# One of two inverse matmuls per class replaced by DMA swaps and an addition from batch 2 on, and new steps for the spectral stages

## The chip, the core and the metric

The kernel runs on one core of one Trainium2 chip. The metric is the device time in microseconds (us). The kernel before took 840.69 us (median of 3 runs, 840.57 to 841.27).

## The reference, cut to what matters

```python
# x: (8, 3008, 256) float32; filt_r, filt_i: (1505, 256)
X = np.fft.rfft(x, axis=1)
Y = X * (filt_r + 1j * filt_i)[None]
y = np.fft.irfft(Y, n=3008, axis=1)            # the spectral part, per batch
h = y.reshape(24064, 256) @ w_in               # 256 -> 2048
g = h + np.sin(alpha * h) ** 2 / (alpha + 1e-9)
out = g @ w_out                                # 2048 -> 256: the MLP part
```

## The kernel before: the parts that the change touches

A transform of 3008 = 47 x 64 points is done as matmuls in three stages per batch: stage 1 (`pa`), a DFT over the 47; a trip through DRAM that turns the data round (store `d1` from `t1`, load `t2`); stage 2, for each of 24 classes a forward matmul (`pb`), the filter, an inverse matmul (`pc`); again a trip through DRAM (`d2` from `g`, load `t4`); stage 3 (`pd`), which gives `y`. The MLP runs in 47 chunks of at most 512 columns, 8 steps a chunk. A step is two hidden tiles (`ph`, two 512-column matmuls each), cosine on ScalarE (`cos`), the activation on VectorE (`v`), and eight output matmuls (`po`) of the chunk before. The spectral pieces of batches 1 to 7 are laid between these steps, so that they hide under the MLP. What is written at one step is called a piece. A matmul's result stands in PSUM, TensorE's output memory, until ScalarE or VectorE copies it out; that copy is called an evacuation.

```python
def stage2(u):                       # 13 pieces; two classes in each
    if u < 12:
        ps = ...                     # PSUM
        for i in range(2):
            s = 2 * u + i
            nc.tensor.matmul(out=ps[:, i, :], lhsT=d_t[:, s, :], rhs=st["t2"][s // 6][:, s % 6, :], ...)
        xf = xfpool.tile([128, 2, C], FP16, ...)
        nc.scalar.copy(out=xf, in_=ps)
        for k in range(2):           # real and imaginary filter
            pt = ppool.tile(...)
            nc.vector.tensor_tensor(out=pt, in0=xf, in1=f_t[k][:, 2 * u:2 * u + 2, :], op=ALU.mult)
            pr.append(pt)
        st["p", u] = pr
    if u > 0:
        w = u - 1
        for i in range(2):
            for k in range(2):       # two inverse matmuls per class
                nc.tensor.matmul(out=ps[:, i, :], lhsT=e_t[:, k, 2 * w + i, :], rhs=pr[k][:, i, :],
                                 start=(k == 0), stop=(k == 1))
        evac(...)                    # 1 in 3 on VectorE, else ScalarE
        # ... every third piece: store g to d2

# the step at which each piece is written; pending pieces are sorted by it
plan = {1: [-45 + i for i in range(8)],
        2: [-29 + 14 * i / 13 for i in range(13)],
        3: [-10, -9] + [-7 + 2 * i for i in range(14)]}      # plus 48 * b
```

The lines on an engine do not stand in program order: a scheduler orders them at build time by its own estimate of when each is ready. Each engine then works through its list in that order.

## Time and profile before

| | before |
|---|---|
| time, median | 840.69 us |
| TensorE (PE) busy | 799.8 us, 96% |
| VectorE (DVE) busy | 628.1 us, 75% |
| ScalarE (ACT) busy | 613.0 us, 73% |

The table of 20 us windows has for each engine the busy us in the window with the number of instructions, then the granted TensorE clock, the DMA engines' busy share and GB/s. These windows hold stages 1 and 2 of one batch:

```profile
core 0: us, PE busy (x) PEld busy (x) DVE busy (x) ACT busy (x) POOL busy (x), PEclk, DMA share, GB/s
160.00:180.00 20.00, 19.79 (x137) 12.58 (x135) 14.74 (x24) 16.17 (x34) 1.55 (x3) 1.00 0.60 120
180.00:200.00 20.00, 20.00 (x155) 13.84 (x154) 15.51 (x26) 15.18 (x31) 0.52 (x1) 1.00 0.78 179
200.00:220.00 20.00, 19.89 (x147) 14.17 (x145) 17.62 (x36) 16.15 (x32) 0.00 (x0) 1.00 0.33 76
```

TensorE has no room there; VectorE in stage 2 (200 to 220) is at 88%.

The chain that ended last, as shares of the span by engine and then by line, from the page of the kernel before:

```profile
PE 83%; DMA 7%; ACT 4%; issue 3%; DVE 2%; POOL 0%; SPq 0%; ACTq 0%; DVEq 0%; POOLq 0%
PE po L369 36%; PE ph L354 35%; PE pc L199 4%; PE pa L157 3%; ACT cos L357 2%; PE pd L219 2%; PE pb L180 2%; DMA t<-d 1%; DMA w_out<-in_moe_w_out_dram 1%; DMA d<-g 1%; DMA d_t<-d_tbl 1%; DVE p L187 1%; DMA x<-in_x_dram 1%; DMA filt<-in_filt_i_dram 1%; ACT t L135 1%
```

Most of it, 83%, is TensorE, the two MLP products (`po`, `ph`) alone 71%. The groups of instructions (busy us, mean ns, then the idle time before them and what ended most of it) show what the change goes after:

```profile
L199 PE MATMUL pc<-p,e_t 128*128 128x256 f16 x384 | 59.7, 275 | 2.6 <-DVE p L187 1.5
```

A matmul's listed 275 ns is not its cost, because matmuls overlap. The cost in a busy stream is the distance from one matmul's start to the next: median 109 ns for 128x256 and 216 ns for 128x512, worked out from the start times in the trace. The Trainium skill, "TensorE: Matmul & The Clock Gate", section "Wait — 56ns, not 53.3ns?", gives N / 2.4 GHz plus about 2.5 ns for such a distance. Worked out from that formula, an estimate for N = 256 and 512 is 109.2 and 215.8 ns; the trace agrees. From these distances I made a tally: each distance less the median of its shape is lost time, put down to whatever ended TensorE's idle time before the later matmul.

### The profile page before, as it was taken

Reading aid. Unit: us, or ns where it says so; the run is one execution under the profiler, and the core shown is the slowest. Engines: PE = TensorE matmul, PEld = TensorE weight load, DVE = VectorE, ACT = ScalarE, POOL = GpSimd, SP = SyncE. Lnnn points to the kernel's source line nnn. Section 1 sums busy time; section 2 is a strip of 40 time slices with the busy share of each in tenths; the row PEclk is TensorE's granted clock in tenths of the full one; section 3 lists DMA queues with packets and bytes.
Section 4 is the critical chain, followed back from the end, with each engine's and each line's share of the span. In section 5 each row is a group of like instructions: output and inputs, shape, how many; then the busy total and the mean of one; then the engine's idle time right before and its main releaser. Section 6 shows DMA issues by size and latency. Waiting matters only on the chain.

```text
span 837.2 us, 16122 instructions
## 1 busy us (share of the span) xinstructions
PE 799.8 (96%) x5793; PEld 544.2 (65%) x5793; DVE 628.1 (75%) x1119; ACT 613.0 (73%) x1200; POOL 28.3 (3%) x55
## 2 busy tenths in 40 slices
PE   5758999999999999999999999999999999999996
PEld 2425676667776677666776677666777677666674
DVE  3658886778877788777877788777877778777772
ACT  4536886787868787787877777777877878677763
POOL 3210000000000000000000000000000000000000
PEclk9969999999999999999999999999999999999999
DMA  9985835185344744266242763447443353421111
GB/s 220 218 255 117 200 89 130 51 174 116 82 135 81 171 99 109 75 141 153 65 130 60 165 137 82 115 91 171 92 96 94 97 113 83 115 58 38 38 40 45
DMA packets 93495, 94.98 MB, mean 113 GB/s; under 512 B 8084, under 2 KB 82852, under 8 KB 93416
## 3 DMA queue, kind: packets, MB, share of 16 engines
q1 hardware_dynamic: 84784, 75.02, 34.5%
q0 software_dynamic: 6704, 18.09, 12.5%
q10 hardware_dynamic: 1928, 0.86, 0.5%
q8 instruction: 45, 0.74, 0.3%
q14 instruction: 34, 0.28, 0.1%
HBM read 58.02 MB, written 49.81 MB: 129 GB/s over the span
## 4 chain that ended last, share of the span: by engine, by line
PE 83%; DMA 7%; ACT 4%; issue 3%; DVE 2%; POOL 0%; SPq 0%; ACTq 0%; DVEq 0%; POOLq 0%
PE po L369 36%; PE ph L354 35%; PE pc L199 4%; PE pa L157 3%; ACT cos L357 2%; PE pd L219 2%; PE pb L180 2%; DMA t<-d 1%; DMA w_out<-in_moe_w_out_dram 1%; DMA d<-g 1%; DMA d_t<-d_tbl 1%; DVE p L187 1%; DMA x<-in_x_dram 1%; DMA filt<-in_filt_i_dram 1%; ACT t L135 1%
## 5 line engine op out<-in xcount | busy, mean ns | idle before, releaser
L358 DVE SCALAR_TENSOR_TENSOR v<-cos,ph 128x512 f16<-128x512 f32 (+1 forms) x768 | 484.0, 672 | 164.0 <-ACT cos L357 163.5
L357 ACT ACTIVATE cos<-ph 128x512 f32<-128x512 f32 (+1 forms) x768 | 411.6, 589 | 153.9 <-PE ph L354 152.5
L369 PE MATMUL po<-w,v 128*128 128x256 f16 x3008 | 400.9, 273 | 2.6 <-DVE w L337 2.6
L354 PE MATMUL ph<-y,w 128*128 128x512 f16 (+1 forms) x1536 | 391.5, 377 | 0.2 <-ACT y L135 0.2
L369 PEld LDWEIGHTS <-v 128*128 128x128 f16 x3008 | 289.0, 98 | 80.9 <-issue 8.7
L354 PEld LDWEIGHTS <-w 128*128 128x128 f16 x1536 | 150.4, 98 | 101.0 <-issue 4.6
L187 DVE TENSOR_TENSOR p<-xf,filt 128x512 f16<-128x512 f16 x192 | 72.1, 419 | 4.9 <-ACT xf L183 4.5
L375 ACT COPY o<-po 128x512 f32<-128x512 f32 x96 | 55.6, 579 | 17.7 <-PE po L369 15.5
L135 ACT CAST t<-pa 96x512 f16<-96x512 f32 x89 | 51.0, 589 | 19.0 <-PE pa L157 18.9
L183 ACT CAST xf<-pb 128x512 f16<-128x512 f32 x96 | 57.0, 595 | 8.1 <-PE pb L180 5.5
L219 PEld LDWEIGHTS <-t 96*128 96x128 f16 x512 | 36.3, 100 | 39.8 <-DMA t<-d 11.8
L199 PE MATMUL pc<-p,e_t 128*128 128x256 f16 x384 | 59.7, 275 | 2.6 <-DVE p L187 1.5
L157 PE MATMUL pa<-x,wf_t 94*96 94x512 f16 x128 | 47.2, 408 | 10.1 <-DMA x<-in_x_dram 6.3
L219 PE MATMUL pd<-wi_t,t 96*128 96x94 f16 x512 | 43.4, 208 | 11.1 <-DMA t<-d 10.9
L135 ACT CAST y<-pd 128x376 f16<-128x376 f32 x82 | 39.1, 479 | 12.5 <-PE pd L219 12.5
L199 PEld LDWEIGHTS <-e_t 128*128 128x128 f16 x384 | 37.6, 99 | 15.6 <-issue 7.1
L180 PE MATMUL pb<-t,d_t 128*128 128x256 f16 x192 | 38.2, 283 | 2.5 <-DMA t<-d 1.5
L135 ACT CAST g<-pc 128x512 f16<-128x512 f32 x64 | 38.7, 605 | 1.6 <-PE pc L199 1.6
L137 DVE CAST t<-pa 96x512 f16<-96x512 f32 x39 | 26.6, 683 | 15.8 <-PE pa L157 15.8
L180 PEld LDWEIGHTS <-d_t 128*128 128x128 f16 x192 | 18.9, 101 | 23.8 <-issue 4.6
L118 POOL DMA_DIRECT2D x<-in_x_dram x32 | 16.7, 524 | 502.8 <-PE pa L157 490.5
L157 PEld LDWEIGHTS <-wf_t 94*96 94x96 f16 x128 | 16.6, 129 | 19.6 <-issue 9.9
(28 smaller groups left out, 94.3 us busy)
## 6 DMA issues: line engine op xcount, KB each, us to landing
d<-t SPq DMA_DIRECT2D x32, 384.0 KB
d<-g SPq DMA_DIRECT2D x64, 192.0 KB
t<-d SPq DMA_DIRECT2D x32, 384.0 KB
x<-in_x_dram POOLq DMA_DIRECT2D x32, 376.0 KB, 6.9
t<-d SPq DMA_DIRECT2D x60, 192.0 KB
out_dram<-o SPq DMA_DIRECT2D x72, 94.0 KB
w_in<-in_moe_w_in_dram POOLq DMA_DIRECT2D x2, 1024.0 KB, 9.2
w_out<-in_moe_w_out_dram POOLq DMA_DIRECT2D x1, 2048.0 KB, 11.6
```

Source lines behind the costliest of these rows:

```text
L135: marks["act"] = nc.scalar.copy(out=dst, in_=src)
L157: marks["pe"] = nc.tensor.matmul(out=ps[0:NK, :], lhsT=wf_t, rhs=st["x"][ch][:, n0:n0 + 2, :], start=True, stop=True)
L180: nc.tensor.matmul(out=ps[:, i, :], lhsT=d_t[:, s, :], rhs=st["t2"][s // 6][:, s % 6, :], start=True, stop=True)
L183: nc.scalar.copy(out=xf, in_=ps)
L187: marks["prod", u] = nc.vector.tensor_tensor(out=pt, in0=xf, in1=f_t[k][:, 2 * u:2 * u + 2, :], op=ALU.mult)
L199: nc.tensor.matmul(out=ps[:, i, :], lhsT=e_t[:, k, 2 * w + i, :], rhs=pr[k][:, i, :], start=(k == 0), stop=(k == 1))
L219: nc.tensor.matmul(out=psv[:, i, :], lhsT=st["t4"][:, 4 * half + i, cb * 128:cb * 128 + 128], rhs=wi_t, start=True, stop=True)
L354: nc.tensor.matmul(out=ps[:, 0:n], lhsT=w1[:, cb, jb * 128:jb * 128 + 128], rhs=y_cols[:, cb, c0:c0 + n], start=(cb == 0), stop=(cb == 1))
L357: nc.scalar.activation(out=cs[:, 0:n], in_=ps[:, 0:n], func=AFT.Sin, bias=float(np.pi / 2))
L358: marks["snake"] = nc.vector.scalar_tensor_tensor(out=v[k][:, jb, 0:n], in0=cs[:, 0:n], scalar=-1.0, in1=ps[:, 0:n], op0=ALU.add, op1=ALU. ...
L369: nc.tensor.matmul(out=pso[k][:, t % 2, :], lhsT=v[k][:, jb, 128 * t:128 * t + 128], rhs=w2[:, jb, :], start=(jb == 0), stop=(jb == 15))
L375: nc.scalar.copy(out=o[:, 0:nb, :], in_=pso[k][:, 0:nb, :])
```

## The change

The second inverse matmul of a class has the same weights as the first, with their halves swapped and one half negated. So the two matmuls on `xf * f0` and `xf * f1` can be one on `xf * f0 + swap(xf) * f1'`, where `f1'` holds the swapped, signed filter. The change does that from batch 2 on. The halves of `xf` (real and imaginary, partitions 0 to 63 and 64 to 127) are swapped by two DMAs from GpSimd's queue, in the program's order two pieces ahead of VectorE's use. Stage 2 is spread over 24 steps instead of 14, one evacuation in five instead of one in three goes to VectorE, which has the additions to do, and the load of the next batch's x is written behind the t2 load.

```diff
 def stage2(u):                                  # batches 2 to 7; 15 pieces
+    if u < 12:
+        forward(u)
+        xs = xspool.tile([128, 2, C], FP16, ...)
+        for p in range(2):
+            nc.gpsimd.dma_start(out=xs[64 * p:64 * p + 64, :, :],
+                                in_=st["xf", u][64 - 64 * p:128 - 64 * p, :, :])
+        st["xs", u] = xs
+    w = u - 1
+    if 0 <= w < 12:
+        st["p", w] = [product(0, w)]
+    w = u - 2
+    if 0 <= w < 12:
+        xs = st["xs", w]
+        nc.vector.tensor_tensor(out=xs, in0=xs, in1=f_t[1][:, 2 * w:2 * w + 2, :], op=ALU.mult)
+        nc.vector.tensor_tensor(out=st["p", w][0], in0=st["p", w][0], in1=xs, op=ALU.add)
+    w = u - 3
+    if 0 <= w < 12:
+        inverse(w)                              # one matmul per class
...
-        flip[0] = (flip[0] + 1) % 3
+        flip[0] = (flip[0] + 1) % 5
...
 def stage3(u):
     if rest == 0:                               # t4 now loaded one chunk ahead
+        for c in ([0, 1] if ch == 0 else [ch + 1] if ch < 3 else []):
+            load_t4(c)
...
-    plan = {1: [-45 + i ...], 2: [-29 + 14 * i / 13 ...], 3: [-10, -9] + [-7 + 2 * i ...]}
+    def at_step(b, stage, i):                   # stage 0 is the load of x
+        if b == 1 and stage < 3:
+            return 6 + i if stage == 1 else 21 + i
+        return 48 * b - 4 * (b % 2) + (-72 if stage == 0 else -50 + i if stage == 1
+                                       else -36 + 24 * i / 14 if stage == 2
+                                       else -6 + i if i < 4 else -1 + 2 * (i - 4))
```

(Cut: the filter and weight tables in their swapped, signed form, and batches 0 and 1, which keep two matmuls per class.) From the last step of stage 1 (-38 before, -43 after, for even batches) to the first of stage 2 (-29, -36) nine steps have become seven.

More of the change, by code (lines that the diff above doesn't have):

```diff
@@ L22 @@
 NK = 4 * NS
+FUSED = 2
 def dft_tables():
@@ L93 @@
     ppool = pool("pp", 4)
+    xspool = pool("xs", 3)
     gpool = pool("gp", 4)
@@ L149, in stage1 @@
             ch, half = divmod(u, 2)
-            if u == 0:
+            if u == 0 and b < 2:
                 st["x"] = load_x(b)
@@ L171, in stage1, with forward @@
                     st["t2"].append(t2)
+        def forward(u):
+            ps = (ops if b == 0 else fps).tile([128, 2, C], FP32, name=f"pb_{b}_{u}",
+                                               tag="o" if b == 0 else "f")
+            for i in range(2):
+                s = 2 * u + i
+                nc.tensor.matmul(out=ps[:, i, :], lhsT=d_t[:, s, :],
+                                 rhs=st["t2"][s // 6][:, s % 6, :], start=True, stop=True)
+            xf = xfpool.tile([128, 2, C], FP16, name=f"xf_{b}_{u}", tag="xf")
+            nc.scalar.copy(out=xf, in_=ps)
+            st["xf", u] = xf
@@ new lines, in product, with inverse @@
+        def product(k, u):
+            pt = ppool.tile([128, 2, C], FP16, name=f"p_{b}_{u}_{k}", tag="p")
+            marks["prod", u] = nc.vector.tensor_tensor(out=pt, in0=st["xf", u],
+                                                       in1=f_t[k][:, 2 * u:2 * u + 2, :], op=ALU.mult)
+            return pt
+        def inverse(w):
+            pr = st.pop(("p", w))
+            if w % 3 == 0:
+                st["g"] = gpool.tile([128, 6, C], FP16, name=f"g_{b}_{w}", tag="g")
+            ps = fps.tile([128, 2, C], FP32, name=f"pc_{b}_{w}", tag="f")
+            for i in range(2):
+                for k, pt in enumerate(pr):
+                    nc.tensor.matmul(out=ps[:, i, :], lhsT=e_t[:, k, 2 * w + i, :],
+                                     rhs=pt[:, i, :], start=(k == 0), stop=(k == len(pr) - 1))
+            i0 = 2 * (w % 3)
+            evac(st["g"][:, i0:i0 + 2, :], ps, i0 != 2 if b == 0 else None)
+            if w % 3 == 2:
+                for p in range(2):
+                    a0 = p * NS + 6 * (w // 3)
+                    nc.sync.dma_start(out=d2[a0:a0 + 6, :, :].rearrange("s n c -> n s c"),
+                                      in_=st["g"][64 * p:64 * p + 64, :, :])
@@ L173, in stage2, with stage2_first @@
+        def stage2_first(u):
+            if u < 12:
+                forward(u)
+                st["p", u] = [product(k, u) for k in range(2)]
+            if u > 0:
+                inverse(u - 1)
         def stage2(u):
             if u < 12:
-                ps = (ops if b == 0 else fps).tile([128, 2, C], FP32, name=f"pb_{b}_{u}",
-                                                   tag="o" if b == 0 else "f")
-                for i in range(2):
-                    s = 2 * u + i
-                    nc.tensor.matmul(out=ps[:, i, :], lhsT=d_t[:, s, :],
-                                     rhs=st["t2"][s // 6][:, s % 6, :], start=True, stop=True)
@@ L182, in stage2 @@
-                xf = xfpool.tile([128, 2, C], FP16, name=f"xf_{b}_{u}", tag="xf")
-                nc.scalar.copy(out=xf, in_=ps)
-                pr = []
-                for k in range(2):
-                    pt = ppool.tile([128, 2, C], FP16, name=f"p_{b}_{u}_{k}", tag="p")
-                    marks["prod", u] = nc.vector.tensor_tensor(out=pt, in0=xf, in1=f_t[k][:, 2 * u:2 * u + 2, :],
-                                                               op=ALU.mult)
-                    pr.append(pt)
@@ L190, in stage2 @@
-                st["p", u] = pr
-            if u > 0:
-                w = u - 1
-                pr = st.pop(("p", w))
-                if w % 3 == 0:
-                    st["g"] = gpool.tile([128, 6, C], FP16, name=f"g_{b}_{w}", tag="g")
-                ps = fps.tile([128, 2, C], FP32, name=f"pc_{b}_{w}", tag="f")
-                for i in range(2):
-                    for k in range(2):
-                        nc.tensor.matmul(out=ps[:, i, :], lhsT=e_t[:, k, 2 * w + i, :],
-                                         rhs=pr[k][:, i, :], start=(k == 0), stop=(k == 1))
-                i0 = 2 * (w % 3)
-                evac(st["g"][:, i0:i0 + 2, :], ps, i0 != 2 if b == 0 else None)
-                if w % 3 == 2:
-                    for p in range(2):
-                        a0 = p * NS + 6 * (w // 3)
-                        nc.sync.dma_start(out=d2[a0:a0 + 6, :, :].rearrange("s n c -> n s c"),
-                                          in_=st["g"][64 * p:64 * p + 64, :, :])
+                forward(u)
@@ new lines, in stage2 @@
+                xs = xspool.tile([128, 2, C], FP16, name=f"xs_{b}_{u}", tag="xs")
+                for p in range(2):
+                    nc.gpsimd.dma_start(out=xs[64 * p:64 * p + 64, :, :],
[9 more added lines that the diff above has]
+                nc.vector.tensor_tensor(out=st["p", w][0], in0=st["p", w][0], in1=xs, op=ALU.add)
@@ L209, in stage3, with load_t4 @@
+            w = u - 3
+            if 0 <= w < 12:
+                inverse(w)
+        def load_t4(ch):
+            st["t4", ch] = t4pool.tile([NK, 8, C], FP16, name=f"t4_{b}_{ch}", tag="t4")
+            marks["t4"] = nc.sync.dma_start(out=st["t4", ch], in_=d2_rows[:, 8 * ch:8 * ch + 8, :])
         def stage3(u):
@@ L212, in stage3 @@
             if rest == 0:
-                t4 = t4pool.tile([NK, 8, C], FP16, name=f"t4_{b}_{ch}", tag="t4")
-                marks["t4"] = nc.sync.dma_start(out=t4, in_=d2_rows[:, 8 * ch:8 * ch + 8, :])
-                st["t4"] = t4
+                for c in ([0, 1] if ch == 0 else [ch + 1] if ch < 3 else []):
+                    load_t4(c)
             ps = fps.tile([128, 4, 128], FP32, name=f"pd_{b}_{u}", tag="f")
@@ L219, in stage3 @@
                 nc.tensor.matmul(out=psv[:, i, :],
-                                 lhsT=st["t4"][:, 4 * half + i, cb * 128:cb * 128 + 128],
+                                 lhsT=st["t4", ch][:, 4 * half + i, cb * 128:cb * 128 + 128],
                                  rhs=wi_t, start=True, stop=True)
@@ L223, in stage3 @@
             evac(y[:, cb, b % 2, n0:n0 + 4, :], psv)
+        if b >= 2:
+            pieces.append((0, lambda: st.update(x=load_x(b))))
         for u in range(8):
             pieces.append((1, lambda u=u: stage1(u)))
-        for u in range(13):
-            pieces.append((2, lambda u=u: stage2(u)))
+        for u in range(13 if b < FUSED else 15):
+            pieces.append((2, lambda u=u: (stage2_first if b < FUSED else stage2)(u)))
         for u in range(16):
@@ L266, in dup_filter @@
         gs = slice(6 * g, 6 * g + 6)
-        for k in range(2):
-            ins = nc.vector.tensor_copy(out=f_t[k][64:128, gs, :], in_=f_t[k][0:64, gs, :])
+        for ins in (nc.vector.tensor_copy(out=f_t[0][64:128, gs, :], in_=f_t[0][0:64, gs, :]),
+                    nc.vector.tensor_scalar(out=f_t[1][0:64, gs, :], in0=f_t[1][64:128, gs, :],
+                                            scalar1=-1.0, scalar2=None, op0=ALU.mult)):
             behind(ins, marks["prod", 3 * g - 2] if g else s1_dve)
@@ L275 @@
                 ins = nc.gpsimd.dma_start(
-                    out=f_t[k][32 * q:32 * q + 32, 6 * g:6 * g + 6, :],
+                    out=f_t[k][64 * k + 32 * q:64 * k + 32 * q + 32, 6 * g:6 * g + 6, :],
                     in_=bass.AP(tensor=filt.tensor, offset=filt.offset + off,
@@ L287 @@
         behind(nc.scalar.mul(e_t[:, 0, gs, :], pse, 0.125), s1_act)
-        nc.vector.tensor_copy(out=e_t[0:64, 1, gs, :], in_=e_t[64:128, 0, gs, :])
-        nc.vector.tensor_scalar(out=e_t[64:128, 1, gs, :], in0=e_t[0:64, 0, gs, :],
-                                scalar1=-1.0, scalar2=None, op0=ALU.mult)
+        for p in range(2):
+            nc.vector.tensor_scalar(out=e_t[64 * p:64 * p + 64, 1, gs, :],
+                                    in0=e_t[64 - 64 * p:128 - 64 * p, 0, gs, :],
+                                    scalar1=-1.0, scalar2=None, op0=ALU.mult)
     ones = cpool.tile([128, 128], FP32)
@@ L391, in store @@
             p += cnt
-    plan = {1: [-45 + i for i in range(8)],
-            2: [-29 + 14 * i / 13 for i in range(13)],
-            3: [-10, -9] + [-7 + 2 * i for i in range(14)]}
+    def at_step(b, stage, i):
[4 more added lines that the diff above has]
+                                       else -6 + i if i < 4 else -1 + 2 * (i - 4))
     pending = [(1 + i % 4 + 8 * (i // 4), 0, piece) for i, (_, piece) in enumerate(first[25:])]
     for b in range(1, B):
-        at = {1: 0, 2: 0, 3: 0}
+        at = {0: 0, 1: 0, 2: 0, 3: 0}
         for stage, piece in spectral(b):
-            at_step = 48 * b + plan[stage][at[stage]]
-            if b == 1 and stage < 3:
-                at_step = 8 + at[stage] if stage == 1 else 23 + at[stage]
+            pending.append((at_step(b, stage, at[stage]), b, piece))
             at[stage] += 1
-            pending.append((at_step, b, piece))
     pending.sort(key=lambda p: p[0])
```

## The prediction

> **What bounds the kernel now.** TensorE. The table of 20 us windows shows it busy 19.8 to 20.0 us in nearly every window from 80 to 820 us, at granted clock 1.00. Busy is not peak rate, so I took start-to-start distances of matmuls from the trace: median 109 ns for 128x256, 216 ns for 128x512. The Trainium skill, "TensorE: Matmul & The Clock Gate", "Wait — 56ns, not 53.3ns?", gives N/2.4 GHz plus about 2.5 ns; these agree. Time over the medians is about 35 us before 80 us and about 8 us in all after it; largest is a wait of 1.8 us at 142.8 us for batch 1's stage 3 load. So in the steady part a removed matmul is time gained, unless something new stalls TensorE.
>
> **What changes.**
> - Removed: 24 inverse matmuls in each of 6 batches, 144 x 109 ns = 15.7 us, all on the critical path.
> - Batch 1's stages 1 and 2 start two steps earlier: most of the 1.8 us wait should go.
> - VectorE: 72 more 128x512 f16 adds (419 ns each, 335 back to back), 24 to 30 us; evacuations go from one in three to one in five there, about 41 leaving (roughly 26 us) for ScalarE (20 to 24 us).
> - Added: 144 swaps of 64 KB by the GpSimd queue.
> - Early: w_out's load waits for a second stage 3 load; batch 1's x is used sooner. Loss: 0 to 2 us.
>
> **Does another engine take over?** From back-to-back distances (estimates): stage 2 covers 24 steps, about 47.7 us of TensorE; VectorE needs about 43 us of it (90%; before, 27.3 of 32.2 us, 85%, and windows measure 86 to 87%). Stage 1: ScalarE 89% (before 83%, measured 84%). Tight.
>
> **The risk is the swap's latency.** In the built order VectorE's multiplication of the swapped tile stands only one MLP step (two v tiles, about 2 us) behind the evacuation it came from, not two pieces. A GpSimd DMA issue takes 516 ns in the trace, two in a row; the Trainium skill, "DMA: Bandwidth & Descriptors", "Anatomy of one DMA — SWDGE (gpsimd) path", gives about 2.0 us fixed; the shortest x landing here, 4.8 us for 376 KB, allows it. My estimate is 3 us, more beside stores. VectorE works in order, so it idles about 1 us per piece, then catches up; four hidden PSUM buffers give 1.5 to 2 us of slack. I expect 1.5 us of TensorE stall in total, perhaps 10 if swaps take 5 us.
>
> **Prediction.** 840.7 - 15.7 - 1.6 + 1 (early) + 1.5 (new stalls) = 825.9 us, 1.8% faster. Range 821.5 to 834. Chances: faster by over 2% 0.27, within 2% 0.69, slower by over 2% 0.04.
>
> **What would show each step.** Inverse matmuls 240 instead of 384 at unchanged distances: the period of a pair of batches drops from 194.6 us to about 189.4. The waits list shows VectorE waiting for the DMA xs<-xf, landing near 3 us, and hidden matmuls waiting little for v. The wait before batch 1's stage 3 is under 0.5 us. ScalarE busy near 636 us, VectorE near 630.
>
> **What would make it wrong.** Swaps landing after 4 us or more: TensorE stalls at hidden matmuls in each stage 2, 830 to 845 us. Stage 2's inputs arriving late (7 steps after stage 1, not 9): waits at the forward matmuls. ScalarE saturating in stage 1. Below 822 the early part must shrink too.

## More of the kernel before

How the input of stage 2 arrives is seen in the timeline of SyncE's DMA queue and of TensorE (start us, us, line, output<-input; rows in between are cut). `d<-t` is the `d1` store; `t<-d` is the `t2` load, which waits for the store to land. Buffer numbers are left out of names.

```profile
start us, us, engine line op out<-in xcount [idle before <-releaser]
177.53 4.81 SPq L161 DMA_DIRECT2D d<-t  x2
187.89 5.32 SPq L169 DMA_DIRECT2D t<-d  x8
196.60 0.38 PE L180 MATMUL pb<-t,d_t 128*128 128x256 f16 x2
```

The first of these lines covers two stores, the second of which was issued at 182.03. The load could be issued 5.9 us after it, and the first forward matmul ran at 196.60 without a wait. Over batches 2 to 6 it is 5.6 to 8.8 us from the last store to the load's issue; for batch 7, which has no x loads beside it, 3.0. In the waits list, forward matmuls wait for the load once, in batch 0:

```profile
PE pb L180 <- DMA t<-d: 1.5, 1, 1.5
```

## The result, and the profile after

The changed kernel took 866.07 us (median of 4 runs, 865.59 to 866.83) against 840.92 us. The ratio is 1.030, with a 95% interval of 1.028 to 1.032. Ratios here are the mean time of one kernel's runs over that of the other's of the same rounds, so not quite the ratio of the medians quoted. It is slower by 3%, where 1.8% faster was predicted.

The same windows of the changed kernel (they are at slightly different points of the program, but again in batch 2):

```profile
core 0: us, PE busy (x) PEld busy (x) DVE busy (x) ACT busy (x) POOL busy (x), PEclk, DMA share, GB/s
160.00:180.00 20.00, 19.86 (x143) 12.88 (x141) 14.02 (x23) 16.56 (x34) 1.55 (x3) 1.00 0.78 177
180.00:200.00 20.00, 17.71 (x126) 11.74 (x124) 12.25 (x23) 13.44 (x27) 3.15 (x6) 0.91 0.63 141
200.00:220.00 20.00, 18.87 (x137) 13.17 (x135) 16.26 (x34) 15.79 (x32) 6.23 (x12) 1.00 0.38 85
```

Stage 1 (160 to 172) is as full as before. In stage 2 TensorE, VectorE and ScalarE all do less: nobody took over, all wait, and the clock fell in one window. The chain that ended last says for what:

```profile
PE 56%; DMA 21%; DVE 9%; ACT 7%; issue 5%; SPq 1%; POOL 1%; ACTq 0%; DVEq 0%; POOLq 0%
PE po L406 24%; PE ph L391 24%; DMA xs<-xf 8%; DMA d<-t 6%; DVE v L395 5%; DMA t<-d 4%; ACT cos L394 3%; PE pa L159 3%; PE pc L200 2%; ACT t L137 2%; DMA w_out<-in_moe_w_out_dram 2%; PE pb L181 1%; PE pd L252 1%; DVE p L189 1%; ACT xf L184 1%
```

DMA went from 7% of the chain to 21%: the swaps (`xs<-xf`), the `d1` stores (`d<-t`) and loads (`t<-d`). In the groups the inverse matmuls are 240 and no longer 384:

```profile
L200 PE MATMUL pc<-p,e_t 128*128 128x256 f16 x240 | 44.2, 279 | 8.0 <-DVE g L139 4.1
```

The waits list (who waited for whom: us in total, times, longest us) has, among others:

```profile
DVE xs L233 <- DMA xs<-xf: 41.7, 28, 3.8
PE pb L181 <- DMA t<-d: 16.7, 6, 4.0
PE ph L391 <- DVE v L395: 11.0, 8, 1.9
PE pc L200 <- DVE g L139: 4.1, 4, 1.7
```

There are two separate stories in these four lines.

**The t2 load is late.** Forward matmuls (`pb`) stood for it six times, once of them in batch 0. SyncE's queue and TensorE in batch 2 (rows in between are cut):

```profile
start us, us, engine line op out<-in xcount [idle before <-releaser]
172.51 0.32 SPq L163 DMA_DIRECT2D d<-t  x1
181.71 5.28 SPq L171 DMA_DIRECT2D t<-d  x8
186.17 0.44 PE L181 MATMUL pb<-t,d_t 128*128 128x256 f16 x2 [2.29 <-DMA t<-d]
```

Now 9.2 us pass from the last store to the load's issue, and the forward matmul ran at 186.17, 4.5 us later, after a wait of 2.3 us. In batches 2 to 6 it is 9.1 to 9.9 us, against 5.6 to 8.8 before. GpSimd's queue shows that the x loads of the next batch were issued among the stores, as in the kernel before (166.37 to 180.57 there), and not behind the t2 load; nothing in the change makes them wait for it:

```profile
start us, us, engine line op out<-in xcount [idle before <-releaser]
157.94 0.52 POOL L120 DMA_DIRECT2D x<-in_x_dram  x1 [69.02 <-PE po L406]
162.68 0.52 POOL L120 DMA_DIRECT2D x<-in_x_dram  x1 [4.22 <-PE pa L159]
167.42 0.52 POOL L120 DMA_DIRECT2D x<-in_x_dram  x1 [4.22 <-PE po L406]
172.16 0.52 POOL L120 DMA_DIRECT2D x<-in_x_dram  x1 [4.22 <-PE pa L159]
187.51 1.07 POOL L224 DMA_DIRECT2D xs<-xf  x2 [14.84 <-ACT xf L184]
```

**VectorE stands for the swap.** From the timeline of VectorE, in the same batch:

```profile
216.22 1.28 DVE L395 SCALAR_TENSOR_TENSOR v<-cos,ph 128x512 f16<-128x512 f32 x2
220.41 0.43 DVE L233 TENSOR_TENSOR xs<-xs,filt 128x512 f16<-128x512 f16 x1 [2.91 <-DMA xs<-xf]
220.75 1.28 DVE L395 SCALAR_TENSOR_TENSOR v<-cos,ph 128x512 f16<-128x512 f32 x2
```

and of TensorE:

```profile
218.91 1.04 PE L406 MATMUL po<-w,v 128*128 128x256 f16 x8
221.48 1.19 PE L391 MATMUL ph<-y,w 128*128 128x512 f16 x4 [1.53 <-DVE v L395]
```

The `v` tiles that would have freed hidden PSUM buffers stand behind the waiting multiplication in VectorE's list, so after 2.91 us of it TensorE runs out of PSUM and loses 1.53 us. The trace gives for all 144 swaps, from issue to landing:

```profile
DMA to landing us min/median/max: 1.8/3.0/5.8
```

The tally of lost TensorE time after 80 us of the span:

| lost for | before | after |
|---|---|---|
| forward matmul waits for the t2 load | 0 | 15.0 us |
| granted clock at half | 0 | 5.7 us |
| hidden matmul waits for v (VectorE behind the swap) | 0.2 us | 12.2 us |
| inverse matmul waits for an evacuation on VectorE | 1.2 us | 7.1 us |
| everything else, each part small | 13.0 us | 14.7 us |
| sum | 14.4 us | 54.7 us |

The sum rose by 40.3 us, the part before 80 us by 2.7 us (34.6 to 37.3), and the removed matmuls are worth 15.7 us: 40.3 + 2.7 - 15.7 = 27.3 us, as much as the spans of the two profiles differ, 864.5 - 837.2 = 27.3 us. (A recount from the traces gives sums up to 0.6 us lower, and the same difference.) So the places are found. What the tally can't tell is cause: whether the two losses are one, and whether the swap, its place in VectorE's order, or VectorE's work is to blame.

### The profile page after: what moved, and what is told of

Its sections match the earlier page's. It is cut to its first block, busy times and chain, and to the rows that moved or that the text cites. A ratio compares the mean times of both kernels' runs of the same rounds, so it can differ in the third digit from the quotient of the medians.

```text
span 864.5 us, 16214 instructions
## 1 busy us (share of the span) xinstructions
PE 793.9 (92%) x5649; PEld 531.9 (62%) x5649; DVE 625.1 (72%) x1146; ACT 634.1 (73%) x1245; POOL 104.2 (12%) x199
## 3 DMA queue, kind: packets, MB, share of 16 engines
q0 software_dynamic: 11312, 27.54, 17.2%
## 4 chain that ended last, share of the span: by engine, by line
PE 56%; DMA 21%; DVE 9%; ACT 7%; issue 5%; SPq 1%; POOL 1%; ACTq 0%; DVEq 0%; POOLq 0%
PE po L406 24%; PE ph L391 24%; DMA xs<-xf 8%; DMA d<-t 6%; DVE v L395 5%; DMA t<-d 4%; ACT cos L394 3%; PE pa L159 3%; PE pc L200 2%; ACT t L137 2%; DMA w_out<-in_moe_w_out_dram 2%; PE pb L181 1%; PE pd L252 1%; DVE p L189 1%; ACT xf L184 1%
## 5 line engine op out<-in xcount | busy, mean ns | idle before, releaser
L224 POOL DMA_DIRECT2D xs<-xf x144 | 75.0, 525 | 309.5 <-ACT xf L184 306.2
L137 ACT CAST t<-pa 96x512 f16<-96x512 f32 x98 | 56.6, 593 | 17.3 <-PE pa L159 17.2
L233 DVE TENSOR_TENSOR xs<-xs,filt 128x512 f16<-128x512 f16 x72 | 30.5, 423 | 42.1 <-DMA xs<-xf 41.7
L189 DVE TENSOR_TENSOR p<-xf,filt 128x512 f16<-128x512 f16 x120 | 48.1, 420 | 17.6 <-ACT xf L184 17.4
L137 ACT CAST y<-pd 128x376 f16<-128x376 f32 x107 | 51.5, 482 | 10.1 <-PE pd L252 10.0
L181 PE MATMUL pb<-t,d_t 128*128 128x256 f16 x192 | 38.5, 284 | 17.7 <-DMA t<-d 16.7
L200 PE MATMUL pc<-p,e_t 128*128 128x256 f16 x240 | 44.2, 279 | 8.0 <-DVE g L139 4.1
L137 ACT CAST g<-pc 128x512 f16<-128x512 f32 x75 | 45.7, 609 | 4.7 <-PE pc L200 4.6
L200 PEld LDWEIGHTS <-e_t 128*128 128x128 f16 x240 | 23.7, 100 | 19.4 <-issue 10.1
```

Of the source, the lines that this page charges most:

```text
L137: marks["act"] = nc.scalar.copy(out=dst, in_=src)
L189: marks["prod", u] = nc.vector.tensor_tensor(out=pt, in0=st["xf", u], in1=f_t[k][:, 2 * u:2 * u + 2, :], op=ALU.mult)
L224: nc.gpsimd.dma_start(out=xs[64 * p:64 * p + 64, :, :], in_=st["xf", u][64 - 64 * p:128 - 64 * p, :, :])
```

## The experiments

Two theories that may both hold: **T**, the inputs of stage 2 are late because its distance from stage 1 was cut; **S**, the swap's latency, seen from VectorE's order, stalls VectorE and through it TensorE. Rivals: **W**, VectorE and ScalarE have too much work in stage 2; and that one of T and S is only the other's shadow.

Medians, with ratios to the runs of the kernel before on the same chip:

| run | us | ratio (95% interval) |
|---|---|---|
| changed kernel | 866.07 | 1.030 (1.028 to 1.032) |
| e1 before, half of the inverse left out | 826.68 | 0.984 (0.982 to 0.985) |
| e2 stage 1 three steps earlier | 847.05 | 1.009 (1.006 to 1.012) |
| e3 no swap DMAs | 846.40 | 1.007 (1.004 to 1.010) |
| e4 schedule without the fused inverse | 860.04 | 1.025 (1.022 to 1.028) |
| e5 multiplication two pieces behind | 847.83 | 1.009 (1.006 to 1.012) |
| e6 both repairs | 829.65 | 0.987 (0.985 to 0.989) |
| e7 x loads behind the swaps | 882.40 | 1.048 (1.045 to 1.051) |
| e8 e2 with swaps from SyncE | 850.42 | 1.012 (1.010 to 1.013) |
| e9 e6 with batch 0's t4 loads as before | 826.15 | 0.983 (0.982 to 0.985) |
| e10 e9 with the inverse one piece later | 822.33 | 0.978 (0.977 to 0.980) |
| e11 e6 again, beside e9 and e10 | 827.92 | 0.985 (0.983 to 0.986) |

### e1: what a removed matmul is worth

```diff
-                    for k in range(2):
+                    n = 2 if b < 2 else 1
+                    for k in range(n):
```

(in the kernel before, with `stop` at `n - 1`; the result is wrong)

> The kernel before with the second inverse matmul of each class left out from batch 2 on, all else as before (its result is wrong on purpose). It measures the term of my sum that the whole gain rests on. If a removed matmul is worth its start-to-start distance, 144 x 109 ns = 15.7 us go: about 825 us, ratio 0.981. Rival: part of it turns into waits for VectorE or ScalarE, because TensorE then runs ahead of them in stage 2: 830 us or more.

826.68 us against 840.37 us: 13.7 of the 15.7 us came. The rest went to somewhat longer waits (the tally after 80 us is 16.7 us instead of 14.4) and to the part before 80 us (1.8 us more). So the base of the prediction's sum holds, and nothing in taking the matmuls away makes the loss.

### e2: stage 1 earlier

```diff
-    -50 + i if stage == 1
+    -53 + i if stage == 1
```

> The changed kernel with stage 1 of batches 2 to 7 three MLP steps earlier (ten steps from its start to its last t2 load's use instead of seven). Theory T (stage 2's inputs are late): the waits of the forward matmuls for the t2 load, 15.0 us in the changed kernel's trace, and the 5.7 us at half clock behind them go: about 846 us. Theory S (the swap's latency alone makes the loss, the t2 wait is only where TensorE happens to stop): the stall moves to hidden matmuls, 860 us or more.

847.05 us: 19 us gained. In the tally the waits for the t2 load fell from 15.0 to 0.6 us and the half clock from 5.7 to 1.7 us; the waits of hidden matmuls for `v` stayed at 12.2 us and those of inverse matmuls at 7.2 us. T is a loss of its own, and S is not its shadow.

### e3: no swap

```diff
-                for p in range(2):
-                    nc.gpsimd.dma_start(out=xs[64 * p:64 * p + 64, :, :], in_=st["xf", u][...])
...
-    nc.vector.tensor_tensor(out=xs, in0=xs, in1=f_t[1]...)
+    nc.vector.tensor_tensor(out=xs, in0=st["xf", w], in1=f_t[1]...)
```

(also four `xf` and two `xs` buffers instead of three and three; wrong)

> The changed kernel with the swap DMAs left out: VectorE multiplies the unswapped tile (its result is wrong on purpose), same VectorE and TensorE work. Theory S: with nothing to wait for, the waits of hidden matmuls for v (12.2 us) and of inverse matmuls for an evacuation (7.1 us) go, about 20 us: 846 us, with the t2 waits left at 15 to 20 us. Rival W (VectorE and ScalarE simply have too much work in stage 2 after the adds and the moved evacuations): the waits stay, 860 us or more.

846.40 us: 20 us gained with all of VectorE's multiplications and additions and all of ScalarE's evacuations still there. Hidden matmuls lost nothing for `v` and inverse matmuls nothing for evacuations in the tally; the t2 waits stayed at 15.2 us. W falls. (The scheduler moved the multiplication too, so e3 does not tell the swap from its place in the order; e5 does.)

### e4: the schedule alone

```diff
-FUSED = 2
+FUSED = 8
```

> The changed kernel's schedule (stages' steps, x loads, evacuations one in five on VectorE) without the fused inverse: all batches multiply twice and use two inverse matmuls per class, no swaps. If T and S are two separate losses of about 20 us each, the schedule alone costs T's: about 858 us, with forward matmuls waiting 15 us for t2. If the swaps alone do the harm, also by slowing the t2 loads, this is 841 us or less.

860.04 us. With no swap in the program, the forward matmuls lose 14.7 us for the t2 load and the half clock 7.6 us. So the late input is made by the schedule and not by the swaps.

### e5: the multiplication where the program has it

The order in which VectorE's instructions stand, as built, shows the multiplication of a swapped tile two `v` tiles behind the evacuation it came from, in the changed kernel as in e2. The program writes it two pieces later, 3.4 steps. e5 forces the written order:

```diff
-    nc.vector.tensor_tensor(out=xs, in0=xs, in1=f_t[1][...], op=ALU.mult)
+    behind(nc.vector.tensor_tensor(out=xs, in0=xs, in1=f_t[1][...], op=ALU.mult), marks["snake"])
```

(`marks["snake"]` is the last `v` tile written; `behind` is an order on the engine, not a wait)

> The changed kernel with one order added: VectorE's multiplication of the swapped tile stands behind the last v tile of the MLP step in which it is written in the program, so really two pieces behind its evacuation; nothing else. Theory S says that the distance on VectorE, not the swap as such, costs the 12.2 us at hidden matmuls and most of the 7.1 us at inverse matmuls: about 848 us, with the t2 waits of 15 us left. If the latency has too long a tail for two pieces (over 6.5 us), waits stay: 855 us or more.

847.83 us: the same swaps, landing in 1.8 to 5.7 us as before, cost nothing once VectorE asks for them later. The median time from the evacuation's end to the multiplication went from 4.2 to 7.7 us, and none of the 72 multiplications waited. The hidden matmuls' 12.2 us are gone. In exchange inverse matmuls of batches 2 to 7 lose about 4.5 us for the sum, which now comes later. S is settled: it is the distance in VectorE's order.

### e6 and e11: both repairs

> Both repairs: stage 1 three steps earlier and the multiplication really two pieces behind. If T and S are separate and complete, both losses go (21 + 19 us): about 827 us, ratio 0.983, like the half-inverse kernel. If one repair brings a new loss (the longer distance delays the inverse matmuls and so batch stage 3), 832 us or more.

829.65 us, and correct. Separately the repairs gave 19.0 and 18.2 us, together 36.4 us: the losses add up. The waits list of e6 that answers to the one shown of the changed kernel has no line for the swap any more:

```profile
PE pb L181 <- DMA t<-d: 3.2, 2, 2.6
PE ph L392 <- DVE v L396: 0.5, 1, 0.5
```

(2.6 of the 3.2 us are batch 0's). So repaired, the fused kernel is 1.3% faster than the one before.

> The kernel with both repairs once more, on the chip of the two runs beside it, so that their differences of 3 us can be read: 829.5 us, ratio 0.987.

827.92 us; the same kernel differed by 1.7 us.

### e7: the x loads really behind

That the x loads stand behind the t2 loads was only an order of writing. e7 makes it an order on GpSimd's queue, behind the last swap of the batch before:

```diff
+            if b > FUSED:
+                behind(ins, marks["swap"])
...
-        (-72 if stage == 0
+        (-59 if stage == 0
```

> The changed kernel with the x loads of batch b+1 really behind the t2 loads of batch b: ordered on the GpSimd queue behind the last swap of batch b, from batch 3 on (batch 2's x as before). Theory T in its finer form: the seven steps are too short only because the x loads share the DMA queues with the d1 stores and t2 loads (last store to first t2 issue 9.1 to 9.9 us in the changed kernel, 3.0 us for batch 7 that has no x loads after it). Then the t2 waits go for batches 2 to 7 as at batch 7, the first swaps too land sooner: about 847 us. If the distance of seven steps is itself too short, the waits stay at 10 us or more: 858 us or more.

882.40 us: the worst of all, and still the half of the expectation that was about T came true. SyncE's queue in batch 2:

```profile
start us, us, engine line op out<-in xcount [idle before <-releaser]
174.78 0.32 SPq L165 DMA_DIRECT2D d<-t  x1
177.77 5.28 SPq L173 DMA_DIRECT2D t<-d  x8
```

The load is issued 3.0 us after the last store instead of 9.2, and after batch 0 the forward matmuls lose 0.3 us: seven steps are enough when no x load runs beside. But the x loads now run beside stage 2's stores, and the wait has moved to stage 3:

```profile
PE pd L254 <- DMA t<-d: 37.5, 7, 8.6
DVE xs L235 <- DMA xs<-xf: 37.8, 24, 3.2
```

Stage 3's matmuls lose 29.9 us in the tally and the half clock 10.0 us. I had counted the bytes of the x loads as free in their new place. They are as much in the way there. In batch 2 they were in flight from 229.6 to 242.5, and landed before stage 3's load was issued. What was late is the `d2` store in front of that load. In SyncE's queue it stands behind nine output stores, which took 12.86 us in e7 and 7.92 us in the changed kernel:

```profile
230.19 12.86 SPq L426 DMA_DIRECT2D out_dram<-o  x9
243.17 1.25 SPq L209 DMA_DIRECT2D d<-g  x2
249.10 0.32 SPq L243 DMA_DIRECT2D t<-d  x1
```

```profile
231.89 7.92 SPq L424 DMA_DIRECT2D out_dram<-o  x9
239.93 1.92 SPq L207 DMA_DIRECT2D d<-g  x2
244.56 0.32 SPq L241 DMA_DIRECT2D t<-d  x1
```

(e7 above, the changed kernel below.) The store came 5.3 us after the last evacuation in e7 and 0.3 us after it in the changed kernel; in e7's batch 7, with no x loads beside it, 0.7 us. In the kernel before, x loads ran beside the same stores as in the changed one, and with two more steps of distance no forward matmul after batch 0 waited for the load.

### e8: the swaps from SyncE's queue

```diff
-    nc.gpsimd.dma_start(out=xs[...], in_=st["xf", u][...])
+    nc.sync.dma_start(out=xs[...], in_=st["xf", u][...])
```

(on e2)

> The stage-1-early kernel (847 us) with the swaps issued from SyncE's queue instead of GpSimd's. If the latency is GpSimd's two issues of 0.52 us and its queue, swaps land about 1 us sooner and half of the 19 us at hidden and inverse matmuls goes: about 837 us. If SyncE's queue is held up by stores in front of the swaps, the waits grow: 850 us or more.

850.42 us against e2's 847.05 us: no gain. VectorE still waited 33.8 us for swaps, once for 9.3 us. In SyncE's queue the swaps stand between the stores of the output:

```profile
196.45 6.58 SPq L224 DMA_DIRECT2D xs<-xf  x6
203.14 1.65 SPq L424 DMA_DIRECT2D out_dram<-o  x4
206.28 1.11 SPq L224 DMA_DIRECT2D xs<-xf  x2
```

Whether an otherwise empty hardware queue would be quicker is left open.

### e9 and e10: two further steps

e9 is e6 with batch 0's stage 3 loads one chunk at a time, as in the kernel before:

```diff
-    for c in ([0, 1] if ch == 0 else [ch + 1] if ch < 3 else []):
+    for c in ([ch] if b == 0 else [0, 1] if ch == 0 else [ch + 1] if ch < 3 else []):
```

> The kernel with both repairs, and batch 0's stage 3 loads again one chunk at a time, so that w_out's load waits for one stage 3 load and not for two. In the changed kernel the first output projection waits 4.4 us for w_out's weights (2.6 us before), and a half-clock stretch that follows is 6.8 us long (3.4 us before). If the second load in front is the cause, 1.8 us of wait and about as much at half clock go: about 826.5 us (both repairs alone: 829.65). If the early part merely scatters by a few us between runs, 829 us.

826.15 us, but e11 beside it gave 827.92 us, and the intervals overlap. Worse for the theory, the first output matmul waited 3.5 us for w_out's weights in e9 and 2.3 us in e11, so the wait did not follow the order of the loads; e6 and e11, the same kernel, had 5.4 and 2.3 us. That part scatters between runs; this one is inconclusive.

e10 writes the inverse matmuls one piece later, in 16 pieces over the same 24 steps:

```diff
-    w = u - 3
+    w = u - 4          # and range(16), 24 * i / 15
```

> As the run with the early loads restored, and the inverse matmuls one piece later (16 pieces instead of 15 in the same 24 steps). The 4.5 us that inverse matmuls wait for the sum of the products and small delays there, in the trace with both repairs, should go: 3 to 4 us less than that run, about 823 us. If the denser pieces bring new waits for VectorE, no gain.

822.33 us, correct, 3.8 us less than e9. The inverse matmuls' waits for the sum are gone (the tally after 80 us is 12.3 us, e9's 17.2), and only one multiplication waited for a swap, 0.7 us:

```profile
DVE xs L233 <- DMA xs<-xf: 0.7, 1, 0.7
```

e10 beats both kernels: 2.2% faster than the one before, 43.7 us less than the changed one.

## Why the prediction was wrong, point by point

- **The gain of 15.7 us was right in kind and nearly in size.** e1 gave 13.7 us. With the waits repaired, the period of a pair of batches in e10's trace is 443.7 - 254.4 = 189.3 us, where 189.4 was predicted; in the changed kernel as it is, it was 467.6 - 261.4 = 206.2 us.
- **The failing step is the term "+ 1.5 (new stalls)".** It measured about 40 us, in two parts.
- **First part: stage 2's input, which the sum held at zero.** The prediction names it only among what would make it wrong. It cost 15.0 us of waits and 5.7 us at half clock (e2, e4). Part of it could have been read beforehand: in the kernel before, batch 3's t2 load was issued at 286.03 and its first forward matmul ran at 292.32, so 6.3 us lay between, where the changed kernel's first forward matmul in batch 2 came 4.5 us after that issue. The spare time was about 1.8 us, and two steps, more than 3.5 us, were being taken away. An average over DMA engines (33 to 78% busy in these windows) hid this. But by the same sum batch 5 (6.9 us) would have been about 1 us short, batch 6 (7.7 us) about even, and batches 2 and 4 (8.7 and 9.0 us) not short; yet all five waited, 15.0 us. The rest came because the load was issued later after the last store, 9.1 to 9.9 us instead of 5.6 to 8.8. That this time falls to 3.0 us without x loads beside it is shown by e7; why it grew between the two kernels, which both have them there, is not shown.
- **Second part: the swap's wait, mis-sized.** The latency itself was right: 3.0 us from issue to landing at the median. But VectorE counts from the evacuation's end. In nearly every piece 0.3 us passed to the first issue and 1.3 us to the end of the second, and the 28 multiplications that waited started 3.6 to 7.5 us after it, not 3. The mean wait was no longer than forecast, 41.7 us over 72 pieces or 0.6 us each where about 1 us was expected; it came unevenly, up to 3.8 us at a time. The tail, up to 5.8 us to landing, is what stops TensorE: the slack of four hidden PSUM buffers absorbs a usual wait and not one of 2.9 us. And I left out that evacuations on VectorE are held up by the same wait, which cost the inverse matmuls about 6 us more than before. The prediction had put 10 us on swaps of 5 us; e3 and e5 show 18 to 20 us.
- **Right:** that the built order puts the multiplication one step and not two pieces behind; that this was the risk; ScalarE's busy time (636 predicted, 634.1 measured) and VectorE's (630, 625.1); that neither takes over (W fell in e3); that batch 1's wait before stage 3 goes (0.6 us in the tally after, 1.8 before).
- **Early part:** predicted 1 us of loss (range 0 to 2), measured 2.7. In the other runs this part scatters from 34.3 to 42.8 us with nearly the same early code, so neither number says much.

What is left open: why some swaps take 5 to 6 us to land when the DMA engines are about 40% busy. The changed kernel's trace shows only what they ran beside: the 22 swaps with nothing issued from SyncE in the 3 us before them landed after 1.9 us at the median and 3.4 at most, the ten beside a t2 load after 5.2 us at the median and 4.5 at least; the other slow ones ran beside output stores. No run takes these transfers away one by one.

## What to carry to other kernels

When a stage is moved closer to the one that feeds it, read the spare time of the slowest transfer between them in the trace, batch by batch, before taking steps away; a mean DMA share does not show it. "Two pieces ahead" written in a program is no distance where a scheduler orders each engine's list: look at the built order, count from the producer's end to the consumer's place, and hold the distance to the tail of the latency and not to its median, above all on an engine whose other work frees buffers for the one that bounds the kernel. Moving a load out of one transfer's way can put it in another's: e7 removed one wait and made a greater one.

## What the Trainium skill lacked or had wrong

- "TensorE: Matmul & The Clock Gate", section "What's actually happening", says that the clock falls to half after an idle window of about 3.4 us. Here waits of only 2.0 to 2.9 us came with half clock in 7 of 9 cases, in the traces of the changed kernel, e3, e4 and e5 together, those of 3.1 to 4.2 us in 7 of 8, and ten waits of 1.4 to 1.98 us never. In these four traces a stretch at half clock, after 80 us and before the one at the end, is 3.41 us or twice that, which agrees with the page's window. What decides between waits of one length can be worked out from the kept traces: in each, the half-clock stretches begin on a fixed grid of 3.413 us (to within 2 ns). Of the grid's windows that ran at full clock, from 80 us to 12 us before the end, in all 13 traces, each of the 21 in which TensorE was idle for 2.0 us or more was followed by half clock, and none of the 2793 with less than 1.85 us; of two at 1.91 and 1.96 us the first was. So e3's wait of 3.33 us, split by the grid into 1.70 and 1.64 us, cost no clock, and e4's of 2.01 us, all in one window, did. e4's five waits, 14.7 us, took another 7.6 us at half clock.
- "DMA: Bandwidth & Descriptors", section "Anatomy of one DMA — SWDGE (gpsimd) path", gives about 2 us fixed plus the bytes. For 64 KB that makes 2.15 us, an estimate from the page's fit; the least here was 1.8 us, a little under it. The median of 3.0 and the longest of 5.8 us, beside other transfers, decided this case, and the page has no such figure for an SBUF-to-SBUF transfer.
- The same page's section "SWDGE vs HWDGE vs iDMA" calls the hardware queues faster in setup. The swaps from SyncE's queue (e8) brought no gain, 850.42 us against 847.05; their issues took 0.59 us at the median there and 0.52 us on GpSimd, and they stood behind stores in that queue. The page gives no figure for how long a DMA stands behind others that the same engine issues; VectorE's longest wait for a swap was 9.3 us in e8 and 3.8 in the changed kernel.
